# Two attention state transposes in other PSUM banks, one gating product in two halves, and one group's product order, in a fused attention and feed-forward kernel

## The chip, the cores and the metric

The kernel runs on one core of one Trainium2 chip. Its time is the device time of one execution in microseconds (us); the number compared is the median of several runs.

The core has five engines with queues of their own: TensorE (PE, with its weight loads shown apart as PEld), VectorE (DVE), ScalarE (ACT), GpSimd (POOL) and SyncE (SP, which here issues nearly all DMAs). Matmuls write to PSUM, which this kernel divides into three pools of banks: two banks "at", two banks "h", and four accumulators "o0" to "o3". An engine works through its instructions in program order.

## The reference

Two blocks follow one another, all in float32. The first is a cross attention between tokens and a small set of states, for 8 batches of 8 heads (S = 512 tokens, Ns = 32 states, D = 64):

```python
scores = scale * x @ state.T                   # 512 x 32 for each head
xread = softmax(scores) @ state                # 512 rows of output
sread = softmax(scale * state @ x.T) @ x       # 32 rows of output
out = concatenate([xread, sread], axis=2)
```

The rows of all heads are put side by side into a matrix `X` of 4352 x 512 (544 rows for each batch), and the second block is a feed-forward layer with d_ff = 2048:

```python
h = X @ w_in                                    # 4352 x 2048
g = h * erf(softplus(h))
return g @ w_out                                # 4352 x 512
```

## The kernel before

**Two products become one.** `xread @ w_in` is softmax(scores) @ (state @ w_in). So the kernel first forms `m`, the product of a batch's states with a group of 512 columns of w_in ("mixed", L397 to L424; 128 x 2 x 512), and then the hidden values as `m` times the turned attention weights `aT`. For this the states must stand in `st` both ways: they are loaded as rows, transposed on PE into PSUM and copied back over themselves by ACT. That is `states` (L177): batch 0 alone at the start (L308), batches 1 to 4 and 5 to 7 later (L823 and L824), seven transposes with two copies (L183).

**Order of the work.** d_ff is split into four groups of 512 columns. The 512 tokens of a batch are a set. Set 0 runs while the weights arrive: `convert`, `on_act` and `on_dve` turn pieces of w_in and w_out into the form that the matmuls want, in passes on ACT (L144, L146) and DVE (L147 to L149). Its hidden products are L709 (`first0`, into an "h" bank), its softplus L713, its copy of h L716, its erf L719, its h * erf L722, its output products L549 (`project`, into the accumulators). All this, L747 to L917, is written out by hand line by line, and `in_order` (called at L918) holds the PE, DVE, ACT and SP instructions traced so far in exactly that order.

After L918 the order is the scheduler's. Sets 1 to 7 (`fast`, L642) take two pairs of groups each, and a last one the 256 `sread` rows. `b` is the set, `h` the half (a pair of groups gives the output for one half of the tokens), `k` the group in the pair. Each group's two large products are done as seven smaller products in place of eight (a Strassen scheme):

- `hidden7` (L473): seven products of 512 columns (four matmuls of L493 each), in two "h" banks in turn. DVE adds and ACT copies them (L501, L504, L509) into four blocks c11, c12, c21, c22 of `hs`; ACT then does the softplus of each block into `s` (L500).
- `finish` (L542): erf over all four blocks of `s` on ACT (L543), then `s * hs` on DVE (L544), 128 x 2048 in one instruction. `s` is now the four blocks A11, A21, A12, A22 that the output product needs.
- `project7` (L580): seven products of `s`, and of sums of blocks of `s`, with blocks of w_out and their sums (T1 to T4, formed in `combine_w`, L575), four matmuls (L599) each, into the accumulators. The four sums S1 to S4 are formed on DVE (L595 to L598) and overwrite `hs`. The usual order is 0 to 6; both groups of the first half of set 1 take (0, 1, 6, 3, 2, 5, 4).
- `store7` (L603): after the pair's second group, ACT's copy L610 and five adds on DVE (L609) put the halves together, and SP sends them out.

The products of one group's `project7` are given out a few matmuls at a time (`between`) amid the next group's `hidden7`; `side` hangs other work at numbered steps, among it the next attention's scores (L197), the turned tokens (`turn_x`, L339, fed by the loads of L100), the `sread` product (L277, scaled by L283) and the next mixed groups (`mixed_pair`, L407, copied by L410 and L411). The products are listed as

```python
products = ((A12, B21, 0, 0), (A11, B11, 2, 0), (A22, T[4], 1, 0), (S2, T[2], 0, 1),
            (S3, T[3], 2, 1), (S1, T[1], 1, 1), (S4, B22, 3, 0))
```

with left block, right block, accumulator, and half of the accumulator's columns. In `s`, A11, A21, A12 and A22 are blocks 0, 1, 2 and 3.

Of the kernel before, what the change touches and what calls it, by code (L numbers as in the profile page):

```python
# [8 lines left out]
F32 = mybir.dt.float32  # L9
U32 = mybir.dt.uint32  # L10
ALU = mybir.AluOpType
ACTF = mybir.ActivationFunctionType
# [4 lines left out]
def kernel(  # L17
# [17 lines left out]
    nc = tc.nc  # L35
# [3 lines left out]
    P = 128  # L39
# [4 lines left out]
    GF = 4  # L44
# [14 lines left out]
    ps_at = ctx.enter_context(tc.tile_pool(name="ps_at", bufs=2, space=PSUM))  # L59
    ps_h = ctx.enter_context(tc.tile_pool(name="ps_h", bufs=2, space=PSUM))  # L60
# [47 lines left out]
    for c in range(NC):  # L108
        (nc.scalar, nc.sync)[c % 2].dma_start(
            out=x_t[0][:, c], in_=x[0, :, P * c:P * c + P].rearrange("h p d -> p h d"))  # L110
    for e in range(2):
        nc.sync.dma_start(out=st[:, 0, D * e:D * e + D],
                          in_=state[0].rearrange("(i e) n d -> e i n d", e=2)[e])
# [52 lines left out]
    def warm(n):  # L166

        for _ in range(n):
            last = nc.tensor.matmul(out=spare[:, 0:P], lhsT=ident, rhs=ident, start=True,
                                    stop=True)  # L170
        return last
# [2 lines left out]
    sT = const.tile([P, NK, B, Ns], F32, name="sT")  # L174
    aT = {}

    def states(bs):  # L177


        ps = ps_h.tile([P, len(bs), P], F32, name="h")  # L180
        for k, b in enumerate(bs):
            last = nc.tensor.transpose(out=ps[:, k], in_=st[:, b, :], identity=ident)
        nc.scalar.copy(st[:, bs[0]:bs[-1] + 1, :], ps)  # L183
        return last
# [5 lines left out]
    def scored(b, xT):  # L190


        s2 = [ps_at.tile([P, S], F32, name="at") for _ in range(2)]
        for i in reversed(range(NI)):
            for e in range(2):
                r, q = slice(D * e, D * e + D), slice(Ns * i, Ns * i + Ns)
                on_pe = nc.tensor.matmul(out=s2[e][q, :], lhsT=st[r, b, q], rhs=xT[r, i, :],  # L197
                                         start=True, stop=True)
        marks.append(on_pe)
        return s2  # L200
# [10 lines left out]
    def states_weights(b, sc, both):  # L211

        aT[b] = keep.tile([P, 2, S], F32, name="aT")
        a = both[:, 0:2].rearrange("p e (k n) -> p e k n", n=Ns)
        m1 = small.tile([P, 2, NC * NI], F32, name="m1")
        for e in range(2):
            nc.vector.transpose(out=both[:, e], in_=sc[e])
        for e in range(2):
            nc.vector.reduce_max(out=m1[:, e], in_=a[:, e], axis=AX.X)
        for e in range(2):  # L220
            nc.vector.tensor_tensor(a[:, e], a[:, e], over(m1[:, e]), op=ALU.subtract)
            nc.scalar.activation(out=a[:, e], in_=a[:, e], func=ACTF.Exp, scale=scale)
        return a

    def sums(a):
        z1 = small.tile([P, 2, NC * NI], F32, name="z1")
        for e in range(2):
            nc.vector.reduce_sum(out=z1[:, e], in_=a[:, e], axis=AX.X)
        return z1

    def normalise(a, z1):
        nc.vector.tensor_scalar(z1, z1, 1e-9, None, op0=ALU.add)
        nc.vector.reciprocal(z1, z1)
        for e in range(2):
            nc.vector.tensor_tensor(a[:, e], a[:, e], over(z1[:, e]), op=ALU.mult)

    def largest(sc):
        m2 = small.tile([P, 2], F32, name="m2")
        for e in range(2):
            nc.vector.reduce_max(out=m2[:, e:e + 1], in_=sc[:, e], axis=AX.X)  # L240
        nc.vector.tensor_scalar(m2, m2, -scale, None, op0=ALU.mult)
        return m2

    def weigh_tokens(sc, m2, a2):

        z2 = small.tile([P, 2], F32, name="z2")
        for e in range(2):
            nc.scalar.activation(out=a2[:, e], in_=sc[:, e], func=ACTF.Exp, bias=m2[:, e:e + 1],
                                 scale=scale, accum_out=z2[:, e:e + 1])
        return z2  # L250

    def inverse(z):
        nc.vector.tensor_scalar(z, z, 1e-9, None, op0=ALU.add)
        nc.vector.reciprocal(z, z)

    def turn_weights(a2):
        a2T = att.tile([P, 2, NC, P], F32, name="sc")
        for e in range(2):
            ps = ps_at.tile([P, NC, P], F32, name="at")
            for c in range(NC):  # L260
                nc.tensor.transpose(out=ps[:, c, :], in_=a2[:, e, P * c:P * c + P],
                                    identity=ident)
            nc.scalar.copy(a2T[:, e], ps)
        return a2T
# [27 lines left out]
    def attention0(between):  # L292

        xt = x_t[0]
        xT = att.tile([P, NI, S], F32, name="xT")
        xp = [ps_o.tile([P, S], F32, name="o%d" % i) for i in range(3)]
        xp.append(ps_h.tile([P, S], F32, name="h"))
        for c in 1, 0, 2, 3:  # L300
            if c == 2:
                warm(3)
            for i in range(NI):
                nc.tensor.transpose(out=xp[i][:, P * c:P * c + P],
                                    in_=xt[:, c, 2 * i:2 * i + 2, :], identity=ident)
        for i in range(NI):
            (nc.scalar.copy, nc.vector.tensor_copy)[i % 2](xT[:, i, :], xp[i])
        states(range(1))  # L308
        s2 = scored(0, xT)
        between[0]()  # L310
        both = att.tile([P, NI, S], F32, name="xT")
        sc = att.tile([P, 2, S], F32, name="sc")
        a = states_weights(0, s2, both)
        for e in range(2):
            nc.scalar.copy(sc[:, e], s2[e])
        between[1]()
        z1 = sums(a)
        between[2]()
        normalise(a, z1)
        for e in range(2):  # L320
            nc.vector.transpose(out=aT[0][:, e], in_=both[:, e])

        def rest():
            a2 = both[:, 2:4]
            m2 = largest(sc)
            yield
            z2 = weigh_tokens(sc, m2, a2)
            inverse(z2)
            yield
            a2T = turn_weights(a2)  # L330
            yield
            read_tokens(0, a2T, z2)
            yield

        return rest()
# [203 lines left out]
                          copies[i](hs[:, i], hp), on_pe))  # L539
        return s, hs, banks  # L540

    def finish(s, hs):  # L542
        return (nc.scalar.activation(out=s, in_=s, func=ACTF.Erf),  # L543
                nc.vector.tensor_tensor(s, s, hs, op=ALU.mult))  # L544

    def project(gT, g, acc, rs=range(NC), ts=range(GF)):
        for r in rs:
            for i in ts:
                nc.tensor.matmul(out=acc[r], lhsT=gT[:, i, P * r:P * r + P],  # L549
                                 rhs=w_out[:, GF * g + i, :],  # L550
                                 start=(g == 0 and i == 0),
                                 stop=(g == NG - 1 and i == GF - 1))
                yield
# [80 lines left out]
    def tiles(n):  # L634
        return [ps_o.tile([P, d_model], F32, name="o%d" % r) for r in range(n)]
# [3 lines left out]
    def begins(b):  # L639
        return 1 - b % 2  # L640

    def fast(b, parts, put):  # L642
        for h in range(parts):
            box = []

            def project_(gT, k, g, h, box):
                if k == 0:
                    box.extend(tiles(4))
                yield from project7(*gT, g, k == 0, k == 1, box,
                                    (0, 1, 6, 3, 2, 5, 4) if (b, h) == (1, 0) else range(7))  # L650
                if k == 1:
                    store7(box, put(h))

            def first(g, h, between, *copy):
                gT = hidden7(b, g, h, between, *copy)
                finish(*gT)
                return gT
            for k in range(2):
                g = k ^ h ^ begins(b)
                yield lambda *how, g=g, h=h: first(g, h, *how), \  # L660
                    lambda gT, k=k, g=g, h=h, box=box: project_(gT, k, g, h, box)

    def done(steps):
        for _ in steps:
            pass
# [24 lines left out]
    def on_act(kind, j, ks=range(2)):  # L690
        for k in ks:
            made[kind, j][0][k]()
# [31 lines left out]
    def group():  # L724
        return [act.tile([P, 4, S], F32, name=n) for n in ("s", "hs")]
# [24 lines left out]
    def some0(g, gT, rs, ts):  # L750
        done(project(gT[0], g, acc, rs, ts))
# [38 lines left out]
    g1 = group()  # L790
# [29 lines left out]
    m_t[0, 2] = mix.tile([P, 2, gw], F32, name="m")  # L820
    mixed_part(0, 2, 0, 2, nc.scalar.copy, nc.scalar.copy)
    on_act("o", 4, [1])
    for bs in range(1, 5), range(5, B):  # L823
        states(bs)  # L824
    some0(1, g1, range(1), range(2, 4))
    on_dve("i", 5)
    load_xq(1)
    g2 = group()
# [83 lines left out]
    at = [combine_a(1)]  # L912
# [12 lines left out]
    for b in range(1, B + 1):  # L925
# [4 lines left out]
        for g, (first, second) in enumerate(groups):  # L930
# [32 lines left out]
            copy = [nc.vector.tensor_copy] if (b, g) == (1, 1) else []  # L963
# [43 lines left out]
```

## Time and profile before

| what | before |
|---|---|
| time, median of 7 runs | 734.24 us (734.05 to 734.38) |
| time of the profiled execution | 734.24 us |
| its span in the profile | 732.4 us |
| PE busy | 721.7 us (99%), 5016 matmul records |
| PE weight loads busy | 587.4 us (80%) |
| DVE busy | 524.2 us (72%), 765 instructions |
| ACT busy | 395.6 us (54%), 498 instructions |
| granted PE clock | 1.00 |
| bytes moved | 46.40 MB |

The span runs from the first to the last recorded instruction; the time has some 1.8 us around it. A float32 matmul leaves two records: where the code has 4 matmuls, the trace counts 8. Rows that lie close together are merged in a timeline ("x8"), and a matmul's row includes the way out of the array, so that rows of PE overlap by a little. "[0.47 <-ACT st L183]" after a row is the time its engine was idle before it, and what it waited for. A row's names read out<-in.

By stage (busy us of each engine in a stretch of the span):

| stretch, us | what runs | PE | DVE | ACT |
|---|---|---|---|---|
| 60 to 65 | end of set 0's second group, state transposes | 4.53 of 5 | 4.54 | 5.00 |
| 65 to 89 | set 0's third group, last weights | 24.00 of 24 | 18.76 | 20.25 |
| 89 to 106 | attention of set 1 | 16.63 of 17 | 14.70 | 13.74 |
| 106 to 134 | last products of set 0, set 1's first group | 28.00 of 28 | 22.86 | 16.61 |
| 134 to 147 | set 1's first project7 | 12.64 of 13 | 11.99 | 7.26 |
| 147 to 162 | set 1's second project7 begins | 14.79 of 15 | 15.00 | 8.01 |
| 162 to 172 | its end | 10.00 of 10 | 9.33 | 7.09 |
| 172 to 212 | second half of set 1 | 39.79 of 40 | 29.80 | 20.84 |
| 212 to 732 | sets 2 to 7 and the sread rows | 516.80 of 520 | 352.05 | 251.04 |

### The profile page before, as it was taken

Reading aid. Unit: us, or ns where it says so; the run is one execution under the profiler, and the core shown is the slowest. Engines: PE = TensorE matmul, PEld = TensorE weight load, DVE = VectorE, ACT = ScalarE, POOL = GpSimd, SP = SyncE. Lnnn points to the kernel's source line nnn. Section 1 sums busy time; section 2 is a strip of 40 time slices with the busy share of each in tenths; the row PEclk is TensorE's granted clock in tenths of the full one; section 3 lists DMA queues with packets and bytes.
Section 4 is the critical chain, followed back from the end, with each engine's and each line's share of the span. In section 5 each row is a group of like instructions: output and inputs, shape, how many; then the busy total and the mean of one; then the engine's idle time right before and its main releaser. Section 6 shows DMA issues by size and latency. Waiting matters only on the chain.

```text
span 732.4 us, 12122 instructions
## 1 busy us (share of the span) xinstructions
PE 721.7 (99%) x5016; PEld 587.4 (80%) x5016; DVE 524.2 (72%) x765; ACT 395.6 (54%) x498; POOL 0.7 (0%) x6
## 2 busy tenths in 40 slices
PE   8899999999999999999999999999999999999998
PEld 7334435878889888988989888988898899999996
DVE  4987887997788667867587669866686756675423
ACT  4898894655546444754355445554565434443340
POOL 0000000000000000000000000000000000000000
PEclk9999999999999999999999999999999999999999
DMA  7578842330053202410061104220121000000001
GB/s 234 175 230 227 219 94 58 87 58 30 15 99 67 53 1 55 90 30 30 1 144 23 36 1 93 59 45 9 31 57 30 30 1 30 1 30 1 30 1 29
DMA packets 139166, 46.40 MB, mean 63 GB/s; under 512 B 126696, under 2 KB 130536, under 8 KB 139112
## 3 DMA queue, kind: packets, MB, share of 16 engines
q1 hardware_dynamic: 136840, 44.92, 24.5%
q10 hardware_dynamic: 2272, 0.72, 0.5%
q8 instruction: 39, 0.64, 0.3%
q14 instruction: 15, 0.12, 0.1%
HBM read 33.03 MB, written 8.91 MB: 57 GB/s over the span
## 4 chain that ended last, share of the span: by engine, by line
PE 87%; DVE 5%; ACT 2%; issue 1%; SPq 1%; DMA 0%; DVEq 0%; ACTq 0%
PE o L599 47%; PE h L493 26%; PE o L549 6%; PE at L407 2%; PE h L407 1%; PE h L709 1%; PE at L197 1%; PE at L421 1%; SPq L72 1%; DVE xT L339 1%; PE h L277 1%; DVE s L722 0%; DVE hs L501 0%; PE at L277 0%; DVE hs L716 0%
## 5 line engine op out<-in xcount | busy, mean ns | idle before, releaser
L599 PE MATMUL o<-w_out,s 128*128 128x256 f32 x480 | 118.2, 380 | 0.4 <-DVE s L544 0.4
L599 PE MATMUL o<-raw,hs 128*128 128x256 f32 x480 | 117.3, 382 | 0.0
L500 ACT ACTIVATE s<-hs 128x512 f32<-128x512 f32 x120 | 75.4, 630 | 75.0 <-DVE hs L501 74.6
L599 PE MATMUL o<-w_out,hs 128*128 128x256 f32 x480 | 114.2, 380 | 0.2 <-DVE hs L598 0.2
L599 PEld LDWEIGHTS o<-raw,hs 128*128 128x128 f32 x480 | 89.9, 190 | 22.6 <-issue 10.9
L501 DVE TENSOR_TENSOR hs<-hs,h 128x512 f32<-128x512 f32 x90 | 61.8, 687 | 63.3 <-PE h L493 63.3
L599 PEld LDWEIGHTS o<-w_out,hs 128*128 128x128 f32 x480 | 90.6, 190 | 16.8 <-issue 4.2
L599 PEld LDWEIGHTS o<-w_out,s 128*128 128x128 f32 x480 | 84.6, 191 | 8.5 <-DVE s L544 0.5
L501 DVE TENSOR_TENSOR hs<-s,h 128x512 f32<-128x512 f32 x60 | 41.0, 684 | 67.7 <-PE h L493 67.2
L493 PEld LDWEIGHTS h<-aT,m 128*128 128x128 f32 x672 | 83.8, 192 | 4.3 <-issue 1.4
L493 PE MATMUL h<-aT,m 128*128 128x128 f32 x672 | 84.4, 275 | 0.0
L544 DVE TENSOR_TENSOR s<-s,hs 128x2048 f32<-128x2048 f32 x30 | 68.6, 2286 | 20.4 <-ACT s L543 20.4
L504 ACT COPY s<-h 128x512 f32<-128x512 f32 x29 | 17.0, 585 | 105.0 <-PE h L493 105.0
L549 PE MATMUL o<-w_out,s 128*128 128x512 f32 x128 | 59.0, 600 | 0.6 <-DVE s L722 0.5
L493 PE MATMUL h<-sy,sx 128*128 128x128 f32 x448 | 59.2, 275 | 0.0
L493 PEld LDWEIGHTS h<-sy,sx 128*128 128x128 f32 x448 | 56.5, 192 | 2.0 <-issue 0.5
L543 ACT ACTIVATE s<-s 128x2048 f32<-128x2048 f32 x30 | 57.4, 1912 | 0.3
L509 ACT COPY hs<-h 128x512 f32<-128x512 f32 x29 | 16.9, 584 | 75.0 <-PE h L493 75.0
L599 PE MATMUL o<-raw,s 128*128 128x256 f32 x240 | 56.8, 379 | 0.0
L549 PEld LDWEIGHTS o<-w_out,s 128*128 128x128 f32 x128 | 23.1, 190 | 30.7 <-issue 25.8
L599 PEld LDWEIGHTS o<-raw,s 128*128 128x128 f32 x240 | 43.5, 190 | 4.8
L500 ACT ACT_TABLE_LOAD x31 | 39.8, 1283 | 0.5
(130 smaller groups left out, 913.2 us busy)
## 6 DMA issues: line engine op xcount, KB each, us to landing
raw<-in_moe_w_in_dram SPq DMA_DIRECT2D x8, 1024.0 KB, 5.5
raw<-in_moe_w_out_dram SPq DMA_DIRECT2D x8, 1024.0 KB, 5.1
xq<-in_x_dram SPq DMA_DIRECT2D x112, 64.0 KB, 2.1
x<-in_x_dram SPq DMA_DIRECT2D x56, 128.0 KB, 2.7
out_dram<-ot SPq DMA_DIRECT2D x18, 256.0 KB, 2.1
sc<-xT SPq DMA_DIRECT2D x112, 32.0 KB, 1.9
out_dram<-ot SPq DMA_DIRECT2D x28, 128.0 KB, 1.7
x<-in_x_dram ACTq DMA_DIRECT2D x2, 256.0 KB, 5.6
```

The costliest lines, as they stand in the source:

```text
L72: nc.sync.dma_start(out=t[:, :, h, :], in_=x[b, h].rearrange("(c p) d -> p c d", p=P))
L197: on_pe = nc.tensor.matmul(out=s2[e][q, :], lhsT=st[r, b, q], rhs=xT[r, i, :], start=True, stop=True)
L407: nc.tensor.matmul(out=ps[k][e][q, :], lhsT=st[r, b, q], rhs=w_in[r, 2 * g:2 * g + 2, i, :], start=True, stop=True)
L493: last = nc.tensor.matmul(out=bank[:, q], lhsT=lhsT, rhs=rhs, start=(first and i == 0 and k == 0), stop=(i == GF - 1 and k == len(ops) - 1 ...
L500: nc.scalar.activation(out=s[:, k], in_=hs[:, k], func=ACTF.Softplus)
L501: add = lambda o, x, y: nc.vector.tensor_tensor(o, x, y, op=ALU.add)
L504: copy(m1, p)
L509: copy(c11, p)
L543: return (nc.scalar.activation(out=s, in_=s, func=ACTF.Erf), nc.vector.tensor_tensor(s, s, hs, op=ALU.mult))
L544: nc.vector.tensor_tensor(s, s, hs, op=ALU.mult))
L549: nc.tensor.matmul(out=acc[r], lhsT=gT[:, i, P * r:P * r + P], rhs=w_out[:, GF * g + i, :], start=(g == 0 and i == 0), stop=(g == NG - 1 a ...
L599: nc.tensor.matmul(out=acc[bank][:, E2 * c:E2 * c + E2], lhsT=lhs[:, i, :], rhs=rhs[:, g, i, :], start=(first and i == 0 and c == 0), stop ...
```

## The change

Three places change.

1. `states` takes a pool. Batch 0's transpose stays in the "h" banks; those of batches 1 to 4 and 5 to 7 go into the "at" banks. In the written order they now stand behind the two matmuls of `some0(1, g1, range(1), range(2, 4))`, not in front of them.
2. `finish` takes parts. In the first group of set 1 ((b, h, k) = (1, 0, 0)) the DVE product s * hs is done in two instructions of 128 x 1024: blocks 2 and 3 first, then 0 and 1. ACT's erf stays one instruction.
3. The order (0, 1, 6, 3, 2, 5, 4) is kept for that group alone; the second group of set 1's first half takes the usual order 0 to 6.

```diff
-    def states(bs):
+    def states(bs, pool=ps_at, name="at"):
-        ps = ps_h.tile([P, len(bs), P], F32, name="h")
+        ps = pool.tile([P, len(bs), P], F32, name=name)
...
-        states(range(1))
+        states(range(1), ps_h, "h")
...
-    def finish(s, hs):
-        return (nc.scalar.activation(out=s, in_=s, func=ACTF.Erf),
-                nc.vector.tensor_tensor(s, s, hs, op=ALU.mult))
+    def finish(s, hs, parts=(slice(0, GF),)):
+        nc.scalar.activation(out=s, in_=s, func=ACTF.Erf)
+        for k in parts:
+            nc.vector.tensor_tensor(s[:, k], s[:, k], hs[:, k], op=ALU.mult)
...
-                                    (0, 1, 6, 3, 2, 5, 4) if (b, h) == (1, 0) else range(7))
+                                    (0, 1, 6, 3, 2, 5, 4) if (b, h, k) == (1, 0, 0)
+                                    else range(7))
...
-            def first(g, h, between, *copy):
+            def first(k, g, h, between, *copy):
                 gT = hidden7(b, g, h, between, *copy)
-                finish(*gT)
+                if (b, h, k) == (1, 0, 0):
+                    finish(*gT, (slice(2, 4), slice(0, 2)))
+                else:
+                    finish(*gT)
                 return gT
...
     on_act("o", 4, [1])
+    some0(1, g1, range(1), range(2, 4))
     for bs in range(1, 5), range(5, B):
         states(bs)
-    some0(1, g1, range(1), range(2, 4))
     on_dve("i", 5)
```

What this does to the instruction lists, beside new line numbers (L709 becomes L714, L544 L545, L549 L550, L599 L600, L609 L610):

- PE: the two matmuls of L549 come before the seven transposes. In the group behind set 1's first product, six of L599's matmuls (four on A12, two on A11) now stand after the first two of a hidden product's four matmuls; before, they stood after all four. Ahead of the S4 product stands one matmul of S2's. In the next group the product order is the usual one.
- DVE: the two halves in place of the whole, with the two small L283 between them; then two block sums (S1, S3) ahead of the hidden add that waits for the split product, and the last sum (S4) between the last two hidden adds. In the store of set 1's first half the five adds are mixed with the block sums.
- ACT, SP, POOL and all DMAs: the same instructions in the same order.

## Prediction

> **What bounds the kernel now.** I read the page's chain that ended last first, then the list of waits of TensorE alone, then the timeline around each wait. The chain:
>
> ```profile
> PE 87%; DVE 5%; ACT 2%; issue 1%; SPq 1%; DMA 0%; DVEq 0%; ACTq 0%
> ```
>
> TensorE (PE) carries 87% of the span and is busy in 721.7 of 732.4 us. So an edit counts only by the PE time it closes up, and by whether that gain survives to the end. The waits of PE (who waited for whom, us in total, times, longest) hold one row for each of the three edits:
>
> ```profile
> PE h L709 <- ACT st L183: 0.5, 1, 0.5
> PE o L599 <- DVE s L544: 0.4, 1, 0.4
> PE o L599 <- DVE hs L598: 0.2, 1, 0.2
> ```
>
> Such a row is only the idle part. A matmul row's printed length includes its drain, about 0.16 us that the next row overlaps, and a restarted stream loses about 0.1 us more. So I compare starts with starts. Undisturbed rates, from the chain: 16 records of the hidden products (L493) 1.78 us, so 0.89 for 8; 24 records of L549 10.30 us, so 0.43 each; 8 records of L599 1.73 us, so 0.216 each.
>
> **Part 1: states in the other banks, after two matmuls.** Timeline, start, length, then [idle before <- releaser]:
>
> ```profile
> 60.92 0.66 PE L421 MATMUL at<-w_in,st 64*32 64x256 f32 x16
> 61.51 0.98 PE L182 MATMUL h<-ident,st 128*128 128x128 f32 x7
> 62.33 1.88 PE L549 MATMUL o<-w_out,s 128*128 128x512 f32 x4
> 64.07 0.94 ACT L183 COPY st<-h 128x512 f32<-128x512 f32 x2
> 64.68 1.98 PE L709 MATMUL h<-aT,m 128*128 128x512 f32 x4 [0.47 <-ACT st L183]
> ```
>
> Today the seven transposes take both "h" banks, and the next user of "h", L709, waits until ScalarE (ACT) empties the first, which it can do only after its conversion L146. In the new program order the two matmuls of L549 come first (4 records), then the transposes into "at", then L709. From 61.51: 4 x 0.43 = 1.72 gives 63.23; the transposes take 0.82 (61.51 to 62.33), 64.05; so L709 starts at 64.05 to 64.15 instead of 64.68: **0.55 gained**, between 0.47 (the idle row alone) and 0.63. Two waits are added, both covered. The transposes wait for the "at" banks, which L423 and L424 leave at 62.74 + 0.36 = 63.10, 0.13 before they are wanted. The L421 after L709 (66.59 now, then about 66.04) waits for the two L183 copies, which still start at 64.07 behind L146 and end at 65.01: 1.0 us of cover. Behind that L421 in PE's queue stands all the rest of set 0's third group. L709's "h" banks were last read by L713 at 57.03. No DMA moves and SP's order is the same. The w_in piece issued at 76.20, behind 16 xq issues, does not move with PE; by its median of 5.5 us it lands at 81.7 and is first read at 84.39, so 0.55 earlier still finds it.
>
> **Part 2: one h * erf in two halves.**
>
> ```profile
> 133.41 2.28 DVE L544 TENSOR_TENSOR s<-s,hs 128x2048 f32<-128x2048 f32 x1
> ...
> 134.34 1.06 PE L493 MATMUL h<-sy,sx 128*128 128x128 f32 x8
> 135.75 2.86 PE L599 MATMUL o<-w_out,s 128*128 128x256 f32 x12 [0.36 <-DVE s L544]
> 138.44 1.05 PE L493 MATMUL h<-sy,m 128*128 128x128 f32 x8
> 139.34 1.03 PE L599 MATMUL o<-w_out,s 128*128 128x256 f32 x4
> 140.20 1.05 PE L493 MATMUL h<-aT,sx 128*128 128x128 f32 x8
> ```
>
> From 134.34 to 140.20 PE does 2 x 0.89 + 16 x 0.216 = 5.24 us of work in 5.86: 0.62 is stall. The first product reads block 2 alone (A12), so the upper half is all it needs. A 128x1024 product took 1.23 us (L722 at 59.44), so the half that starts at 133.41 ends at 134.64. The scheduler answers by putting six of L599's matmuls after the first two of L493's four: wanted at 134.34 + 0.45 = 134.79, so no wait is left, by some 0.1. The two small L283 (0.39 from start to next start) now stand between the halves; the second half runs from 134.94 to 136.17 and is wanted at 134.79 + 1.73 = 136.52. What is late next: the split L493 ends 137.8 instead of 135.4, so DVE's add of it (L501, 137.20 now) starts at about 138.05; DVE does the two sums of blocks first, and the last sum (S4) ends near 140.6, wanted 140.9. L493 of 140.20 then starts at 139.6: **0.60 gained**, between 0.36 (the idle row) and 0.62.
>
> The extra cost on VectorE (DVE) is 2 x 1.23 - 2.28 = 0.18 us. It falls where DVE idles: the next L501, at 141.29, shows 1.01 us idle before it, until PE delivered. Uncovered it would leave 732.8. The Trainium skill, "VectorE: DVE Perf Modes", section on the TRN2 errata, speaks against splitting: each instruction pays a fixed latency, and its fp32 formula (N + 151)/0.96 ns would make the split 0.16 us dearer, an estimate from that page; the rows here say 0.18, and uncovered the page's figure would leave 732.8 as well.
>
> Does the gain carry? From 141.29 DVE is full for 26 us (15.00 of 15.00 us from 147 to 162), and PE keeps meeting it: at 158.01 (bank freed by the L501 that ends at 157.96) and at 159.87. So that string must start 0.6 earlier too. Its first member, at 141.29, waits for PE's L493 of 140.20, which does come 0.6 earlier, and every member follows the one before it. So PE and DVE shift alike.
>
> **Part 3: usual order for the second batch's second group.**
>
> ```profile
> 160.81 0.60 PE L599 MATMUL o<-raw,hs 128*128 128x256 f32 x2
> 161.62 1.99 PE L599 MATMUL o<-w_out,hs 128*128 128x256 f32 x8 [0.21 <-DVE hs L598]
> 163.45 0.59 PE L599 MATMUL o<-raw,hs 128*128 128x256 f32 x2
> 163.97 1.09 PE L407 MATMUL at<-w_in,st 64*32 64x512 f32 x16
> ...
> 160.88 0.69 DVE L598 TENSOR_TENSOR hs<-s,hs 128x512 f32<-128x512 f32 x1
> ```
>
> The w_out row needs S4, the last of the four sums, which ends at 161.57. In the usual order the product after 160.8 is A22 by T4; T4 was done by 153.8 and A22 long before, so it starts at once, and S4's product comes last. The stall: 0.81 - 0.43 = 0.38 between the first two starts, and 1.83 - 1.73 = 0.10 of restart in the next: **0.48 gained**, between 0.21 and 0.48. Matmuls are only exchanged. The new order fills bank 3 last, so five store adds (L609 before) now precede the next group's first L501 on DVE, where four did. That add should end near 175.73 - 0.60 = 175.13, and PE needs it at 176.52 - 0.60 - 0.48 = 175.44: 0.3 of cover, beyond which PE waits with that group's last five hidden products behind it.
>
> **Sum.** 0.55 + 0.60 + 0.48 = 1.63; by the low ends 1.04, by the high ends 1.73. After 172 the chain is PE's nearly throughout, and its one excursion over ACT and DVE (202.4 to 211.6) starts from a PE product, so it shifts with it. The profiled execution took 734.24 us (span 732.40, 1.84 around it), the median of the 7 runs too: 734.24 - 1.63 = **732.6**, span 730.8.
>
> **Rivals.**
> 1. *The VectorE string doesn't start earlier.* The chain view leads into it not from PE but over SP's issues from 133.47 and a store's landing at 141.88. If that were a real wait, PE would meet DVE at 158.01 as today and part 2 would be lost: 0.55 + 0.48 = 1.03, 733.2. For it: the chain's own lines. Against: the L501 at 141.29 ended its idle on PE, the next row follows 0.61 later as in an unbroken queue, and its instruction carries no wait.
> 2. *The stalls close only by their idle rows, or the halves hardly help* because the margins of 0.1 in parts 1 and 2 are gone: 1.04, 733.2. For it: those margins are as small as the reading error.
> 3. *Slower: the second half late.* The whole product is now done 0.5 later (136.17 for 135.69), and behind the matmul that reads it stand the rest of the split product and the start of DVE's string. Beyond 136.52 each us late costs one; from about 138.1, when all 1.63 is eaten, the kernel is slower; a half of 3 us would make it about 736. Against: halves of this shape took 1.23.
> That the change doesn't do what it says is ruled out for the order: only these places differ in the instruction lists.
>
> **Numbers.** Forecast 0.62 (its own range 732.2 to 733.0), rival 1 0.18, rival 2 0.15, rival 3 0.05. A measurement of this kernel can tell about 0.2% from no change, 1.47 us, so faster begins below 732.77, inside the forecast's own range: of its 0.62 I give 0.52 to faster and 0.10 to same. Same: 0.10 + 0.18 + 0.15 = 0.43; slower 0.05. The range from 732.2 to 733.6 takes in both bounds of the sum and rivals 1 and 2.
>
> **What would show it.** Right: no idle before the first L709 after the transposes, which starts near 64.1; the first L600 of w_out,s at 134.2 and the L493 in front of DVE's string at 139.05 (both 0.55 earlier still, from part 1); no wait on S4; the next mixed pair's L407 at 162.3 instead of 163.97; span 730.8. Wrong: a wait of PE on ACT near 63.2 or on DVE near 134.2, L339 (144.17 now) at 143.6 instead of 143.0, or a new wait of PE on L501 near 174.9.

## The result and the profile after

The changed kernel takes 732.13 us (median of 15 runs, 732.03 to 732.45) against 734.24 (35 runs, 733.96 to 734.50): ratio 0.9972, 95% interval 0.9966 to 0.9979, or 2.11 us less. The interval lies wholly below 1, so the kernel is faster, as forecast, by some 0.3%; but the median is 0.47 below the forecast 732.6 and 0.07 below the range's low end. Two more series of the same kernel, told below, gave 732.42 and 732.36, that is 1.79 and 1.88 less than the kernel before beside them.

The profiled execution took 732.35 us with a span of 730.5 (before 734.24 and 732.4), so 1.89 less. The chain that ended last, by engine:

```profile
PE 91%; DVE 3%; ACT 2%; issue 1%; DVEq 0%; ACTq 0%
```

PE carries four points more of the span than before. Of PE's waits (engine, line, tile, waited for whom: us in total, times, longest) those of the same hidden and output products (L714, L550, L600) are now:

```profile
PE h L714 <- ACT m L423: 0.5, 1, 0.5
PE o L550 <- DVE s L727: 0.5, 2, 0.3
...
PE h L714 <- ACT s L718: 0.2, 1, 0.2
```

The rows that named L183, L544 and L598 (L183, L545 and L599 now) are gone, and L600 has no row left; the waits that remain come from elsewhere, and stood there before as well.

Part 1's place in the timeline after (start, length, then the group; PEld is a weight load; rows in between are left out, here and below):

```profile
61.58 1.98 PE L550 MATMUL o<-w_out,s 128*128 128x512 f32 x4
62.52 0.36 ACT L423 COPY m<-at 128x256 f32<-128x256 f32 x1
62.97 0.14 PEld L182 LDWEIGHTS at<-ident,st 128*128 128x128 f32 x1 [0.24 <-ACT m L423]
63.40 0.93 PE L182 MATMUL at<-ident,st 128*128 128x128 f32 x7
64.16 1.88 PE L714 MATMUL h<-aT,m 128*128 128x512 f32 x4
65.97 0.66 PE L421 MATMUL at<-w_in,st 64*32 64x256 f32 x16
```

No matmul row has an idle entry: the states' transposes find their bank emptied at 62.88 (62.52 + 0.36), 0.5 us before their first row and 0.09 before its weight load, and L714 starts at 64.16 where it started at 64.68.

Part 2's place:

```profile
132.79 1.22 DVE L545 TENSOR_TENSOR s<-s,hs 128x1024 f32<-128x1024 f32 x1
133.72 0.61 PE L493 MATMUL h<-sy,sx 128*128 128x128 f32 x4
134.16 2.76 PE L600 MATMUL o<-w_out,s 128*128 128x256 f32 x12
134.31 1.22 DVE L545 TENSOR_TENSOR s<-s,hs 128x1024 f32<-128x1024 f32 x1
135.44 0.68 DVE L501 TENSOR_TENSOR hs<-s,h 128x512 f32<-128x512 f32 x1
...
138.96 1.05 PE L493 MATMUL h<-aT,sx 128*128 128x128 f32 x8
140.05 0.69 DVE L501 TENSOR_TENSOR hs<-hs,h 128x512 f32<-128x512 f32 x1 [0.16 <-PE h L493]
```

The first half ends at 134.01 and the first product starts at 134.16 without a wait. The last L501 before the string that keeps DVE full now comes 1.24 us earlier than at 141.29, and DVE idles 0.16 us ahead of it, no longer 1.01.

Part 3's place:

```profile
161.30 1.03 PE L600 MATMUL o<-raw,hs 128*128 128x256 f32 x4
162.26 1.09 PE L407 MATMUL at<-w_in,st 64*32 64x512 f32 x16
167.78 0.38 ACT L611 COPY m<-o 128x256 f32<-128x256 f32 x1
169.17 0.68 DVE L610 TENSOR_TENSOR ot<-m,o 128x512 f32<-128x512 f32 x1
171.96 1.60 PEld L600 LDWEIGHTS o<-w_out,s 128*128 128x128 f32 x8
172.07 1.89 PE L600 MATMUL o<-w_out,s 128*128 128x256 f32 x8
173.80 1.95 PE L493 MATMUL h<-aT,m 128*128 128x128 f32 x16
```

L407 starts 1.71 us earlier than at 163.97, and from there on something more is gained. In the kernel before, the product that answers to the one at 172.07 stood so:

```profile
172.20 0.37 ACT L610 COPY m<-o 128x256 f32<-128x256 f32 x1 [3.07 <-PE o L599]
172.89 1.06 PE L493 MATMUL h<-sy,sx 128*128 128x128 f32 x8
173.07 0.68 DVE L609 TENSOR_TENSOR ot<-m,o 128x512 f32<-128x512 f32 x1
173.80 1.59 PEld L599 LDWEIGHTS o<-w_out,s 128*128 128x128 f32 x8
173.80 1.99 PE L599 MATMUL o<-w_out,s 128*128 128x256 f32 x8
175.63 1.95 PE L493 MATMUL h<-aT,m 128*128 128x128 f32 x16
```

There it started 0.05 after L609, the add that empties accumulator "o0", had ended (173.07 + 0.68 = 173.75). That add also reads `m`, the copy of "o2" that ACT makes from 172.20 to 172.57 (L610), after 3.07 us of waiting for PE to be done with "o2"; on DVE it stands behind the block sums. In the order (0, 1, 6, 3, 2, 5, 4) the last product, 4, goes into "o2"; in the usual order the fifth does, the copy runs at 167.78 and the add at 169.17. The product at 173.80 took 1.83 to the next start, where it takes 1.73 after. Its first weight load shows the same: it starts with the row at 173.80, and 0.11 ahead of it at 171.96 in the changed kernel. That it waited for this bank is read from the rows and was not tried apart. No row of the view calls it a wait, because the long drain of the row at 172.89 (to 173.95) covers it.

**Where the time went, in one table.** ACT's table loads stand one to one in all traces, so the time of one against the same one of before tells how far a kernel has moved by then (us; minus is earlier). The first column is a start offset, from ahead of all three edits: the first matmul of the scores starts between 10.06 and 10.35 us in all the profiles of this study, 2.34 to 2.35 us after the first transposes of x (L304) in every one; in nine of the thirteen the profile has those waiting for the load of x.

| kernel | at 57 | 74 to 134 | 142 to 165 | from 177 to the end | gained by part 1, 2, 3 |
|---|---|---|---|---|---|
| changed kernel | +0.06 | -0.62 | -1.24 | -1.84 | 0.68, 0.62, 0.60 |
| same, second series | +0.16 | -0.53 | -1.15 | -1.75 | 0.69, 0.62, 0.60 |
| same, third series | -0.02 | -0.70 | -1.33 | -1.94 | 0.68, 0.63, 0.61 |
| part 1 alone | +0.05 | -0.61 | -0.60 | -0.61 | 0.66 |
| part 2 alone | +0.16 | +0.15 | -0.47 | -0.47 | 0.62 |
| part 3 alone | -0.08 | -0.07 | -0.07 | -0.67 | 0.60 |

The three gains are steps, each at its own place, and nothing is given back after 177 us. Their sum is 1.90.

### The profile page after: what moved, and what is told of

Read it like the earlier page. It is cut to its first block, busy times and chain, and to the rows that moved or that the text cites. A ratio compares the mean times of both kernels' runs of the same rounds, so it can differ in the third digit from the quotient of the medians.

```text
span 730.5 us, 12128 instructions
## 1 busy us (share of the span) xinstructions
PE 721.6 (99%) x5016; PEld 588.1 (81%) x5016; DVE 524.0 (72%) x766; ACT 395.5 (54%) x498; POOL 0.7 (0%) x6
## 4 chain that ended last, share of the span: by engine, by line
PE 91%; DVE 3%; ACT 2%; issue 1%; DVEq 0%; ACTq 0%
PE o L600 49%; PE h L493 27%; PE o L550 7%; PE at L407 2%; PE h L407 1%; PE h L714 1%; PE at L197 1%; PE at L421 1%; PE h L277 1%; DVE s L727 0%; PE at L277 0%; DVE hs L721 0%; ACT L724 0%; DVE w_out L148 0%; DVE xT L339 0%
## 5 line engine op out<-in xcount | busy, mean ns | idle before, releaser
L600 PE MATMUL o<-w_out,s 128*128 128x256 f32 x480 | 118.0, 380 | 0.0
L600 PE MATMUL o<-raw,hs 128*128 128x256 f32 x480 | 117.3, 382 | 0.0
L600 PE MATMUL o<-w_out,hs 128*128 128x256 f32 x480 | 114.1, 380 | 0.0
L600 PEld LDWEIGHTS o<-raw,hs 128*128 128x128 f32 x480 | 89.9, 190 | 22.6 <-issue 10.9
L501 DVE TENSOR_TENSOR hs<-hs,h 128x512 f32<-128x512 f32 x90 | 61.8, 687 | 62.5 <-PE h L493 62.4
L600 PEld LDWEIGHTS o<-w_out,hs 128*128 128x128 f32 x480 | 90.8, 190 | 16.3 <-issue 4.2
L600 PEld LDWEIGHTS o<-w_out,s 128*128 128x128 f32 x480 | 84.6, 191 | 7.9
L501 DVE TENSOR_TENSOR hs<-s,h 128x512 f32<-128x512 f32 x60 | 41.0, 684 | 67.6 <-PE h L493 67.1
L545 DVE TENSOR_TENSOR s<-s,hs 128x2048 f32<-128x2048 f32 (+1 forms) x31 | 68.7, 2217 | 20.4 <-ACT s L543 20.4
L550 PE MATMUL o<-w_out,s 128*128 128x512 f32 x128 | 59.1, 601 | 0.6 <-DVE s L727 0.5
L600 PE MATMUL o<-raw,s 128*128 128x256 f32 x240 | 56.8, 379 | 0.0
L550 PEld LDWEIGHTS o<-w_out,s 128*128 128x128 f32 x128 | 23.1, 190 | 31.1 <-issue 25.8
L600 PEld LDWEIGHTS o<-raw,s 128*128 128x128 f32 x240 | 43.5, 190 | 4.7
```

The costliest lines, as they stand in the source:

```text
L501: add = lambda o, x, y: nc.vector.tensor_tensor(o, x, y, op=ALU.add)
L545: nc.vector.tensor_tensor(s[:, k], s[:, k], hs[:, k], op=ALU.mult)
L600: nc.tensor.matmul(out=acc[bank][:, E2 * c:E2 * c + E2], lhsT=lhs[:, i, :], rhs=rhs[:, g, i, :], start=(first and i == 0 and c == 0), stop ...
```

## The experiments

The theory: three stalls, removed one by one, whose gains add and carry to the end. The main rivals: a part does nothing by itself, because the DVE string or another wait holds the time, or the gain comes from another piece of the change than the one it was put down to. Edits are against the changed kernel, and line numbers are its own.

**Each part alone, and the whole again.** The kernel before beside these took 734.21 us. Part 1 alone (`p1_states`):

```diff
-                                    (0, 1, 6, 3, 2, 5, 4) if (b, h, k) == (1, 0, 0)
+                                    (0, 1, 6, 3, 2, 5, 4) if (b, h) == (1, 0)
...
-                    finish(*gT, (slice(2, 4), slice(0, 2)))
+                    finish(*gT)
```

> Part 1 alone: the transposes in the at banks and behind the two matmuls; the product s*hs whole, the turned order in both groups. Theory (three separate stalls, each worth its idle plus the restart that follows it): PE ahead by 0.68 us from 72 to the end, 0.58 of it at the L709-like row after the transposes, 733.56 by the median of before. Rival (the gains hang together, because VectorE's full string at 141 to 168 does not move on its own): PE is ahead by 0.6 until 158 and meets the string there, nothing left at the end, 734.2.

Measured: 733.56 (11 runs, 733.39 to 734.03), ratio 0.9991 (0.9982 to 1.0000), so 0.65 less; 0.66 in the trace, all of it by 74 us and kept to the end, so the rival is refuted.

Part 2 alone (`p2_halves`):

```diff
-    def states(bs, pool=ps_at, name="at"):
+    def states(bs, pool=ps_h, name="h"):
...
-                                    (0, 1, 6, 3, 2, 5, 4) if (b, h, k) == (1, 0, 0)
+                                    (0, 1, 6, 3, 2, 5, 4) if (b, h) == (1, 0)
...
-    some0(1, g1, range(1), range(2, 4))
     for bs in range(1, 5), range(5, B):
         states(bs)
+    some0(1, g1, range(1), range(2, 4))
```

> Part 2 alone: the product s*hs of set 1's first group in two halves; states and orders as before. Theory (separate stalls): PE ahead by 0.62 from 140 on, VectorE's string too, the wait for S4 at 161.6 still there at full length, 733.6. Rival (the string starts from a store's landing and not from PE): PE ahead by 0.3 at most at the next scores (L197), nothing left after 162, 734.2.

Measured: 733.63 (11 runs, 733.46 to 733.76), ratio 0.9991 (0.9982 to 1.0000), so 0.58 less; 0.62 in the trace. The wait that part 3 removes is still there in its timeline, and as long:

```profile
161.15 1.99 PE L600 MATMUL o<-w_out,hs 128*128 128x256 f32 x8 [0.21 <-DVE hs L599]
```

It comes 0.47 us earlier than at 161.62, by just what this kernel has gained less its start offset. So the whole DVE string moved with PE, and the prediction's first rival, that it stays where it was, is refuted.

Part 3 alone (`p3_order`) undoes parts 1 and 2: states and place as in the diff just shown, and `finish(*gT)` whole.

> Part 3 alone: usual order in the second group. Theory (separate stalls): the wait for S4 goes, 0.47 at the next mixed pair, and 0.1 more at the first output product of the next group, which finds its accumulator emptied earlier; 0.60 in all, 733.64. Rival (part 3 pays only when part 2 has moved VectorE's string): under 0.2, 734.1 or more, with a new wait of PE on a hidden add (L501) near 175.

Measured: 733.70 (11 runs, 733.53 to 733.82), ratio 0.9993 (0.9984 to 1.0002), so 0.51 less; 0.60 in the trace. By itself this median isn't told apart from no change, and the intervals of parts 1 and 2 just reach 1.0000, so the parts rest on the traces. This one is exact: L407 starts at 163.43, 0.54 earlier of which 0.07 is start offset, so 0.47; the product that waited for the accumulator starts at 173.24 and the next at 174.97, 1.73 later, which gives the rest.

The whole again (`all_again`, no edit):

> The changed kernel again, beside the three parts on one chip. Theory (three separate stalls): the sum of the three parts alone, 1.9 by the trace, 732.3. Rival (something outside the three stalls gives the 0.2 by which the medians differ more than the two profiled executions): 2.1, 732.1, while the three parts alone sum to 1.9 or less.

Measured: 732.42 (8 runs, 732.21 to 732.47), ratio 0.9975 (0.9965 to 0.9985), so 1.79 less. The three parts alone give 0.65 + 0.58 + 0.51 = 1.74. The gains add.

**Part 1 taken apart.** It changes the banks and the place. The kernel before beside this and the next two took 734.26 us. New banks, old place (`s_banks`):

```diff
-    some0(1, g1, range(1), range(2, 4))
     for bs in range(1, 5), range(5, B):
         states(bs)
+    some0(1, g1, range(1), range(2, 4))
```

> The changed kernel with the transposes back in front of the two matmuls, in the at banks. Theory (banks and place are needed together: in the new banks the transposes wait for the copies L423 and L424, which end at 63.1, and nothing stands before them to fill the time): PE idles 1.5 us ahead of the transposes, about 1.6 slower than the changed kernel beside it, 733.9 to 734.0. Rival (the banks alone make the gain, the place is incidental): as the changed kernel, 732.3.

Measured: 733.63 (11 runs, 733.40 to 733.83), ratio 0.9991 (0.9983 to 1.0000). In the trace it stands 1.28 us behind the changed kernel, worse than part 1's old form would be. The transposes now wait for the bank themselves:

```profile
62.64 0.36 ACT L423 COPY m<-at 128x256 f32<-128x256 f32 x1
63.05 0.98 PE L182 MATMUL at<-ident,st 128*128 128x128 f32 x7 [1.25 <-ACT m L423]
```

The wait is the one foreseen, but it ends with L423, the copy that empties the first bank, not with L424: the first four transposes use only that one. That makes it 0.25 shorter than expected (1.25, not 1.5), and the time less than the 733.9 to 734.0 that was expected.

Old banks, new place (`s_place`):

```diff
-    def states(bs, pool=ps_at, name="at"):
+    def states(bs, pool=ps_h, name="h"):
```

> The changed kernel with the transposes behind the two matmuls, but in the h banks. Theory (the copy L183 can't start before 64.1, behind the conversion L146, so the next user of h still starts at 64.7): all of part 1 lost, 0.65 to 0.7 slower than the changed kernel, 733.0. Rival (the place alone makes the gain, since the copies come soon after the transposes): 732.3.

Measured: 733.06 (11 runs, 732.98 to 733.26), ratio 0.9985 (0.9976 to 0.9994), as expected; 0.68 behind the changed kernel in the trace, so part 1 is gone whole:

```profile
64.72 1.98 PE L714 MATMUL h<-aT,m 128*128 128x512 f32 x4 [0.41 <-ACT st L183]
```

The wait for L183 is back. Neither piece alone gains anything; the banks without the place cost 0.6 more than the old form.

**Which half first** (`h_low_first`): the prediction held that the first product needs the upper half.

```diff
-                    finish(*gT, (slice(2, 4), slice(0, 2)))
+                    finish(*gT, (slice(0, 2), slice(2, 4)))
```

> The changed kernel with blocks 0 and 1 of the product s*hs first. The scheduler answers by putting the second product (A11) in front. Theory (one half ready at 134.6 is enough, whichever, as PE has six matmuls to do on it and on the rest of the split product before the other half is wanted at 136.5): as the changed kernel within 0.1, 732.3. Rival (block 2 must come first, because the first product reads it): PE waits 1.0 longer, 733.3.

Measured: 732.53 (11 runs, 732.25 to 732.79), ratio 0.9976 (0.9967 to 0.9985); 0.05 to 0.06 behind the changed kernel in the trace. The scheduler puts the product on the half that is ready (A11) first: it starts at 134.31, 0.15 after that half ended and 1.37 before the other did. So it matters that there are two halves, and hardly which comes first.

**The same cut in set 0's second group** (`v_early`): a product of 128x1024 in two, and, with it, a conversion of ACT moved back behind the copies of `mixed_part`.

```diff
-    times(A, g1)
+    for i in 0, 1:
+        times(slice(i, i + 1), g1)
...
-    on_act("o", 4, [0])
     some0(1, g1, range(NC), range(2))
...
-    on_act("o", 4, [1])
+    on_act("o", 4)
```

> The changed kernel and two edits of the same kinds in set 0's second group: the first product s*hs of 128x1024 (at 52.6) in two of 128x512, and ACT's conversion of a w_out piece (L144 at 61.5) behind the two copies of mixed (L423, L424), so that the at banks are free earlier. Theory (a stall of PE is worth its idle and the restart): PE stops waiting at 53.9, 0.2 + 0.1 gained, and the transposes don't wait in its place; 0.3 faster than the changed kernel, 732.0. Rival (ACT is full from 59 to 65 and takes it back: a wait of PE on L183 or L424 near 63 to 66): 732.3.

Measured: 732.04 (6 runs, 731.92 to 732.11), ratio 0.9970 (0.9959 to 0.9982); 0.35 ahead of the changed kernel in the trace. The place shows in the windows view (stretch: its length, then busy us and number of instructions of PE, PEld, DVE, ACT and POOL, then granted clock, DMA share, GB/s). The changed kernel and, after it, this one:

```profile
53.50:54.00 0.50, 0.41 (x2) 0.08 (x1) 0.50 (x2) 0.50 (x2) 0.00 (x0) 1.00 0.72 139
```

```profile
53.50:54.00 0.50, 0.50 (x2) 0.26 (x2) 0.50 (x2) 0.50 (x2) 0.00 (x0) 1.00 0.72 143
```

A matmul that began at 53.92, just after the whole product's end at 53.86, begins at 53.66, and the L421 behind that row at 60.62, not 60.98: 0.26, and 0.10 of restart. PE's idle time there was only 0.09. All this lies ahead of the conversion that was moved (61.48 in the changed kernel), so the cut alone gave it; what the move adds or saves behind it wasn't tried apart. A second series of this kernel (`v_early2`) ran beside the changed kernel (`all_third`) and the next; the kernel before took 734.24 us there.

> The faster version again, beside the changed kernel on one chip. Theory: 0.35 faster than it, as the first trace had it between 57 and 73 us; 731.9 to 732.1. Rival (the 0.36 of that trace was the start's scatter): within 0.1 of it.

> The changed kernel once more, as the measure for the two beside it. Theory (three stalls, 1.9 in the trace; the rest of any difference between medians is the start, before 21 us, which varies from session to session): 732.1 to 732.5, and in its trace 1.9 between 57 and 177 us. Rival (a fourth gain outside the three): more than 1.9 between 57 and the end.

Measured: 731.97 (6 runs, 731.94 to 732.21), ratio 0.9969 (0.9958 to 0.9981), against 732.36 (9 runs, 732.26 to 732.44), ratio 0.9974 (0.9964 to 0.9984). The ranges don't overlap, and the difference of 0.39 is near that of the traces (0.35): this version beats both kernels. In the third series' trace of the changed kernel the gain is 1.92, all of it at the three places, so there was no fourth.

**Halves in all 30 groups that `first` handles** (`h_everywhere`; 30, not the 31 of the expectation), for the price of a cut by itself:

```diff
-                if (b, h, k) == (1, 0, 0):
-                    finish(*gT, (slice(2, 4), slice(0, 2)))
-                else:
-                    finish(*gT)
+                finish(*gT, (slice(2, 4), slice(0, 2)))
```

> The changed kernel with the product s*hs in two halves (blocks 2 and 3 first) in all 31 groups, not in one. Theory (a further instruction costs VectorE 0.07 us from start to start, and PE only where it meets VectorE's full string): VectorE busy 2 us longer, by the lengths of the rows 5 us; the kernel 0 to 0.2 slower than the changed one. Rival (each further instruction's fixed latency comes out at the end): 2 to 5 us slower.

Measured: 732.47 (9 runs, 732.22 to 732.58), ratio 0.9976 (0.9966 to 0.9985), 0.11 above the changed kernel with ranges that overlap. The traces say as much: by the table loads it has gained 1.79 in all, 0.11 less than the first profile of the changed kernel and 0.13 less than the third. DVE is busy for 525.8 us in 795 instructions, against 524.0 in 766: 1.8 / 29 = 0.062 us for each further one. The kernel loses some 0.06 at each of two places where PE waits for DVE. At 155.76 to 156.73 the hidden products meet the full DVE string: this kernel's rows stand 0.11 ahead of the changed kernel's before (its start was earlier by that) and 0.04 ahead after. And at 210 us PE's wait for L339 is longer by 0.07; the changed kernel, then this one:

```profile
209.77 1.09 PE L197 MATMUL at<-xT,st 64*32 64x512 f32 x16 [0.21 <-DVE xT L339]
```

```profile
209.80 1.09 PE L197 MATMUL at<-xT,st 64*32 64x512 f32 x16 [0.28 <-DVE xT L339]
```

So there is nothing to gain where no PE wait stood, and something to lose, 0.06 a place, where PE waits for DVE already; the other 27 further instructions cost PE nothing that the traces show.

## Why the prediction had the mechanism right and its sum too small

The three stalls closed as forecast, and their gains added. What failed are the sizes of two terms of the sum: part 1 (0.55, measured 0.68) and part 3 (0.48, measured 0.60). Each left out a loss of about 0.10 us in the row behind a wait, so that even the sum of the high ends, 1.73, lay under the 1.90 that the traces show. With the sizes measured the time would still have lain inside the forecast's range (732.34); the median of the first series lies another 0.21 lower, and the cause of this stays open.

- **What bounds the kernel: right.** PE bounds it, and a stall closed in any of the three places shortens the whole. The three idle rows came to 0.47 + 0.36 + 0.21 = 1.04 us and were worth 1.90.
- **Part 1, "0.55 gained", between 0.47 and 0.63: the mechanism right, the size a step that failed; measured 0.68.** The start was right: 64.16 less the start offset 0.06 is 64.10, inside 64.05 to 64.15, which is 0.58. There was luck in it: the two matmuls took 1.82 (61.58 to 63.40) and not 1.72, the transposes 0.76 and not 0.82. What the term left out is the restart in the same row: from L709's start to L421 it was 66.59 - 64.68 = 1.91 before, and is 65.97 - 64.16 = 1.81. That 0.10 was named in the prediction's own rule and counted in parts 2 and 3, but not here. The covers held, but were not those stated. The first four transposes need only L423's bank, empty 0.52 before their row; but their first weight load, which the profile too has waiting for L423, began 0.09 after that. The cover ahead of L421 was 0.87 (65.97 less 65.10), not 1.0. `s_banks` and `s_place` show that both pieces are needed.
- **Part 2, "0.60 gained": right; measured 0.62.** What the step said of the cost on DVE was wrong in size: not 0.18 but 0.07. Two row lengths of 1.22 overlap; from start to start the halves take 1.14 + 1.13 against 2.20 for the whole. It was hidden either way, though of the 1.01 us of DVE's idle time 0.16 is left. `h_everywhere` gives 0.062 for each further instruction. The Trainium skill, "VectorE: DVE Perf Modes", section on the TRN2 errata, fits the lengths of rows; for what an extra instruction costs in a queue, "Perfetto Trace Analysis", section "Optimizing Scalar/DVE Operations", is the one that agrees: about 60 ns of engine time on SBUF, with the length in the profile about twice that overhead, since the other half overlaps the next instruction.
- **"Does the gain carry?": right.** Part 2 alone carries its 0.62 through the DVE string to the end, and in the changed kernel the L339 that was to come at 143.0, not 143.6, starts at 142.93. So rival 1 did not occur.
- **Part 3, "0.48 gained, between 0.21 and 0.48": the other step that failed; measured 0.60.** 0.47 at L407 is what it said. Its upper end looked at the row of S4 alone. A second wait, without an idle entry, stood at 173.80: the next group's first output product waited for the bank that L609 empties at 173.75. In the usual order the accumulator whose copy that add needs is done earlier, the add runs at 169.17, and PE gains 0.11 to 0.13 more, 0.10 of it restart. The prediction looked for a loss among the store's adds and not for a gain. That loss was covered as it said: the L501 behind the five adds ended at 174.44 and PE wanted it at 174.69, 0.25 of cover for 0.3. (The 175.73 from which it worked this out is in no row of the kernel before; that L501 ended at 175.93.)
- **The sum, 1.63 (1.73 at most): too small by 0.27**, 0.13 of it in part 1, 0.02 in part 2 and 0.12 in part 3. With the sizes measured it is 734.24 - 1.90 = 732.34, which is where the changed kernel's profiled execution (732.35) and its other two series (732.42, 732.36) lie.
- **Open: why the first series lies at 732.13**, 0.2 to 0.3 below the other two. Its own profile has no such gain. The start, ahead of anything that the change touches, accounts for the differences between the three profiled executions: the time less the start of the first scores matmul is 732.35 - 10.22 = 722.13, 732.41 - 10.29 = 722.12 and 732.26 - 10.15 = 722.11. By this estimate a run of 732.13 would start that matmul at about 10.0, a little earlier than any profile shows. That this set the median of the first series isn't shown; a difference between chips isn't ruled out either, though the kernel before took 734.24, 734.21 and 734.24 beside the three.
- The second and third rivals did not occur: the gains are nearly twice the idle rows, and the second half, ready at 135.53, stopped nobody.

## What to carry to other kernels

Size a stall from the start of the last undisturbed instruction to the start after the stalled row, never by its idle entry: here 1.04 us of entries were worth 1.90. Having found the wait that an order causes, look for the next user of each bank that the order frees, since a wait can hide under the drain of the row before it. A step that is moved and the banks that it writes belong together: one without the other gained nothing or lost 0.6 us.

## What the runs showed that was not expected

- PE loses about 0.10 us in the row after a stall, besides the stall: 1.91 against 1.81 (four matmuls into h and the way to L421), 1.83 against 1.73 (eight of L600), and 0.10 of the 0.36 in `v_early`. In the timeline such a row is 0.10 longer (1.99 for 1.89, 1.98 for 1.88), and its first weight load starts with it, not 0.11 ahead (173.80 and 173.80, against 171.96 and 172.07). A wait isn't the only thing that does this: in the changed kernel the row at 61.58, behind L421 and without a wait on record, has both marks too (1.98, its load at 61.57).
- An idle time of 0.09 us on PE stood for a loss of 0.36, and none at all for one of 0.11 to 0.13.
- Cutting a DVE product in two costs 0.062 to 0.07 us, though the rows of the halves are 1.22 each and that of the whole 2.28.
- Medians of one kernel in three series differ by up to 0.29 us, as much as half of one of the parts; the traces give the same steps each time within 0.02.
